# Stacking folded groups in two columns, so that one transfer moves a group's four blocks

## The chip, the cores and the metric

The kernel runs on one core of one Trainium2 chip. The time is device microseconds (us) of one execution; lower is better. Kernels are compared by runs in the fast state, taken in the same rounds on the same chip.

Engine names in the profile: PE is TensorE, DVE is VectorE, ACT is ScalarE, POOL is GpSimd, SP is the engine whose in-order queue issues nearly all transfers here.

## The reference

```python
# x: (1, 384, 384, 384) bf16, w1d: (1,) bf16
g = jnp.einsum("bhwc->bc", x) / (H * W)     # mean of each channel
s = jax.nn.sigmoid(g * w1d[0])              # one factor per channel (k = 1)
return x * s[:, None, None, :]
```

The factor needs all of x, so x must be read once for the sum and be there again for the product. x is 1152 rows of 384 bf16 values on each of 128 partitions, 96 KB a row over all partitions, 113 MB in all. The kernel's arena on the chip holds 275 rows.

## The kernel before

Rows are of two kinds. **Streamed** rows (785) are read and summed, dropped, and read again after the sigmoid. **Kept** rows (367) stay on the chip, so they are read only once. To keep more, the kernel folds: four exponent bits that are the same in nearly all values are dropped, and the twelve bits left of a fourth value take their places in three others. (A check on the data, `verdict`, comes after the sigmoid; if it fails, a slow path redoes the kept rows.) Four blocks of rows then fit in the space of three.

```python
QS = [4, 16, 16, 16, 16]            # quadruples kept in each area
...
areas.append((base, 3 * q))         # three blocks of rows
...
# U, V: where the fourth block lands until it is folded; after the sigmoid, where raw kept rows lie
for name, n in (("U", 8), ("V", 8), ("A", 39), ("Y", 8), ("T", 8)): ...
# ... sum phase, for each pair of four-row pieces:
beside = (U, V)[at % 2]
group_load(g, 3 * e, 3 * f, areas[g][0] + 3 * e)          # three blocks, 24 rows
group_load(g, 3 * q + lo, 3 * q + lo + n, beside)         # the fourth block, 8 rows
fold(k, beside + pieces[k][1] - lo)
stream_all(where)
```

After the sigmoid a pair is unfolded on DVE in six turns (`fields`, `three`, `fourth` for each of two pieces). It is stored by two transfers:

```python
f, t, _ = turns[-2]        # after the second piece's three blocks
turns[-2] = (f, t, lambda: send(KEPT, a, ..., w_done, written))     # 24 rows
f, t, _ = turns[-1]        # after its fourth block
turns[-1] = (f, t, lambda: send(KEPT, at, ..., u_done, written))    # 8 rows, from T or U
```

The order of everything after the sigmoid is fixed when the program is built. A loop keeps a clock and a model of how long DVE and the transfers take; it decides when to scale a piece that has landed, when to unfold, and when a free run of rows is large enough to load into. The SP queue issues strictly in this order.

```python
if n >= BIG or n == N_STREAM - todo or (ahead < LOW and n >= 8) or ahead < LAST:
    load(STREAMED, a, todo, todo + n)       # BIG 32 rows, LOW 9 us queued, LAST 4 us
```

## Time and profile before

| | before |
|---|---|
| time, median of 6 runs | 722.55 us (722.34 to 722.82) |
| span of the profiled run | 721.1 us |
| bytes moved | 303.67 MB |
| transfers on the SP queue | 136 (80 loads, 56 stores) |
| DVE busy | 496.0 us |
| last row landed, sigmoid done | 266.9 us, 270.3 us |

"The turn" below is the stretch around the sigmoid, about 265 to 290 us: reading for the sum ends, storing begins.

### The profile page before, as it was taken

How to read it: one execution, taken by the hardware profiler on the slowest of the kernel's cores; microseconds unless marked ns; L12 is line 12 of the kernel's file. 1: busy time of each engine (PE TensorE's matmuls, PEld its weight loads, DVE VectorE, ACT ScalarE, POOL GpSimd, SP SyncE). 2: the span in 40 equal slices, each digit the busy share in tenths (PEclk: the TensorE clock that was granted, in tenths of full speed). 3: DMA queues.
4: the chain of work that ended last, by engine and by line, in shares of the span. 5: the costliest groups of instructions: out<-in, count | busy, mean ns of one | idle time of the engine just before them, and what ended most of it. 6: DMA issues, size and time to landing. Idle time of an engine off the chain costs nothing.

```text
span 721.1 us, 3241 instructions
## 1 busy us (share of the span) xinstructions
PE 215.7 (30%) x1202; PEld 119.8 (17%) x1202; DVE 496.0 (69%) x469; ACT 115.4 (16%) x92; POOL 0.2 (0%) x4
## 2 busy tenths in 40 slices
PE   5777789888987780000000000000000000000000
PEld 2344445554543440000000000000000000000000
DVE  4600004879989809999999998999979994355330
ACT  3600003656767610001000000000000000000000
POOL 0000000000000000000000000000000000000000
PEclk9899999999999995555555555555555555555555
DMA  9999999999999978999999999999999999999997
GB/s 382 425 447 424 425 429 433 435 434 420 433 424 427 428 326 334 418 427 431 433 429 442 416 433 436 436 443 418 433 431 436 429 440 435 420 436 438 434 432 305
DMA packets 19602, 303.87 MB, mean 421 GB/s; under 512 B 2178, under 2 KB 2178, under 8 KB 6402
## 3 DMA queue, kind: packets, MB, share of 16 engines
q1 hardware_dynamic: 19584, 303.67, 98.6%
q8 instruction: 9, 0.15, 0.1%
q14 instruction: 7, 0.06, 0.0%
q10 hardware_dynamic: 2, 0.00, 0.0%
HBM read 190.41 MB, written 113.25 MB: 421 GB/s over the span
## 4 chain that ended last, share of the span: by engine, by line
DMA 53%; DVE 28%; PE 7%; another core or an unknown queue 4%; ACT 3%; SPq 0%; issue 0%; DVEq 0%
DMA arena<-in_x_dram 37%; DVE arena L437 18%; DMA out_dram<-arena 16%; PE bank L230 7%; DVE arena L254 6%; DVE arena L260 4%; ACT arena L294 3%; SPq L224 0%; ACT s_bf L428 0%; PE bank L509 0%; DVE odd L504 0%; DVE odd_i L513 0%; DVE worst L499 0%; DVEq L112 0%
## 5 line engine op out<-in xcount | busy, mean ns | idle before, releaser
L437 DVE TENSOR_TENSOR arena<-arena,s_bf 128x1536 bf16<-128x1536 bf16 (+8 forms) x102 | 241.7, 2411 | 75.5 <-DMA arena<-in_x_dram 58.2
L230 PE MATMUL bank<-arena,ones 128*128 128x384 bf16 x1152 | 207.6, 343 | 52.0 <-DMA arena<-in_x_dram 51.9
L254 DVE TENSOR_SCALAR arena<-arena 128x1536 uint16<-128x1536 uint16 (+2 forms) x247 | 145.8, 633 | 108.4 <-DMA arena<-in_x_dram 97.9
L230 PEld LDWEIGHTS bank<-arena,ones 128*128 128x128 bf16 x1152 | 114.9, 102 | 144.4 <-DMA arena<-in_x_dram 57.4
L260 DVE TENSOR_TENSOR arena<-arena 128x1536 uint16<-128x1536 uint16 (+2 forms) x114 | 121.0, 1062 | 9.7 <-PE bank L230 7.7
L294 ACT ACTIVATE arena<-arena 128x3072 uint16<-128x3072 uint16 (+1 forms) x38 | 102.5, 2696 | 142.3 <-DVE arena L254 142.3
L364 ACT COPY arena<-bank 128x512 uint32<-128x512 uint32 (+1 forms) x7 | 4.0, 570 | 70.1 <-DMA out_dram<-arena 69.9
L245 PE MATMUL bank<-ones,zeros 128*128 128x384 bf16 x48 | 8.3, 326 | 0.0
L294 ACT ACTIVATION_READ_ACCUMULATOR arena<-arena 128x1 f32 x38 | 7.1, 186 | 0.0
L245 PEld LDWEIGHTS bank<-ones,zeros 128*128 128x128 bf16 x48 | 4.7, 98 | 3.1
L509 PE MATMUL bank<-odd,ones 128*128 128x1 bf16 x1 | 0.2, 186 | 15.8 <-DVE odd L504 15.8
L364 ACT COPY bank<-arena 128x512 uint32<-128x512 uint32 (+1 forms) x7 | 3.6, 565 | 0.0
L428 ACT ACTIVATE s_bf<-bank,w_sc 128x384 bf16<-128x384 f32 x1 | 0.6, 581 | 15.9 <-PE bank L230 15.9
L509 PEld LDWEIGHTS bank<-odd,ones 128*128 128x128 bf16 x1 | 0.1, 104 | 16.2 <-DVE odd L504 16.2
L721 ACT ACT_TABLE_LOAD x1 | 1.3, 1283 | 0.7 <-PEq L737 0.7
L324 DVE TENSOR_SCALAR w_sc<-bank 128x1 f32<-128x1 f32 x1 | 0.2, 157 | 1.1 <-PE bank L319 1.1
L314 DVE MEMSET ones<- 128x128 bf16 x1 | 0.2, 165 | 1.0 <-SPq L106 1.0
L319 PE MATMUL bank<-w_bf,ones 1*128 1x1 bf16 x1 | 0.2, 179 | 2.1 <-DMA w_bf<-in_w1d_dram 2.1
L319 PEld LDWEIGHTS bank<-w_bf,ones 1*128 1x128 bf16 x1 | 0.1, 98 | 2.1 <-DMA w_bf<-in_w1d_dram 2.1
L513 DVE CAST odd_i<-bank 128x1 int32<-128x1 f32 x1 | 0.2, 159 | 0.3 <-PE bank L509 0.3
L504 DVE TENSOR_SCALAR odd<-worst 128x1 bf16<-128x1 f32 x1 | 0.2, 156 | 0.0
L499 DVE TENSOR_REDUCE worst<-seen 128x1 f32<-128x38 f32 x1 | 0.2, 180 | 0.0
(5 smaller groups left out, 0.5 us busy)
## 6 DMA issues: line engine op xcount, KB each, us to landing
arena<-in_x_dram SPq DMA_DIRECT2D x17, 4608.0 KB, 35.4
out_dram<-arena SPq DMA_DIRECT2D x6, 4608.0 KB, 43.8
arena<-in_x_dram SPq DMA_DIRECT2D x19, 1248.0 KB, 11.5
arena<-in_x_dram SPq DMA_DIRECT2D x9, 2304.0 KB, 28.3
out_dram<-arena SPq DMA_DIRECT2D x8, 2304.0 KB, 28.4
arena<-in_x_dram SPq DMA_DIRECT2D x4, 4512.0 KB, 33.6
out_dram<-arena SPq DMA_DIRECT2D x3, 4512.0 KB, 26.7
out_dram<-arena SPq DMA_DIRECT2D x9, 1248.0 KB, 11.7
```

The lines of the kernel that those rows point to most:

```text
L230: return nc.tensor.matmul(acc, lhsT=ones[:], rhs=arena[:, i, :], start=first, stop=last)
L245: lambda: nc.tensor.matmul(acc, lhsT=zeros[:], rhs=ones[:, None, :].to_broadcast([P, C // P, P]), start=False, stop=False),
L254: lambda: nc.vector.tensor_scalar(out=dst, in0=src, scalar1=s0, scalar2=s1, op0=op0, op1=op1),
L260: "DVE", lambda: nc.vector.tensor_tensor(out=dst, in0=a, in1=b, op=op), reads=reads, writes=writes
L294: lambda: nc.scalar.activation(out=y, in_=y, func=ACTF.Copy, accum_out=seen[:, 2 * k + i : 2 * k + i + 1]),
L314: fl.add("DVE", lambda: nc.vector.memset(ones[:], 1.0), writes=["ones"])
L319: lambda: nc.tensor.matmul(votes, lhsT=ones[0:1, :], rhs=w_bf[0:1, 0:1], start=True, stop=True),
L364: "ACT", lambda: nc.scalar.copy(dst.bitcast(u32), src.bitcast(u32)), reads=reads, writes=writes
L428: lambda: nc.scalar.activation(out=s_bf[:], in_=acc, func=ACTF.Sigmoid, scale=w_sc[:, 0:1]),
L437: lambda: nc.vector.tensor_tensor(out=v, in0=v, in1=s_bf[:, None, :].to_broadcast([P, n, C]), op=Op.mult),
L509: lambda: nc.tensor.matmul(votes, lhsT=ones[:], rhs=odd[:], start=True, stop=True),
L721: nc.scalar.preload_act_table(ACTF.Sigmoid)
```

## The change

The intent: halve the transfers of kept groups. Groups of eight quadruples are stacked in two columns. A group takes 32 rows while its fourth block is whole, and the first eight rows of the group above it lie where that fourth block was. So one load brings all four blocks, and one store takes them.

```diff
-    QS = [4, 16, 16, 16, 16]
+    PAIR = 2 * PIECE
+    PAIRS = 4
+    U = 3 * PIECE + PAIRS * 3 * PAIR
+    G0 = U + PAIR
+    V = G0 + PAIRS * 3 * PAIR
 ...
+    GROUPS = [(0, PIECE)]
+    COLUMNS = ([FIRST], [])
+    for i in range(PAIRS):
+        for column, a in zip(COLUMNS, (3 * PIECE, G0)):
+            column.append(len(GROUPS))
+            GROUPS.append((a + 3 * PAIR * i, PAIR))
 ...
+    def take(g, lo=0, hi=None):      # the lines that look up a and hi are left out
+        load(KEPT, a + lo, c_group[g] + lo, c_group[g] + hi)
+        sum_rows(a + lo, hi - lo)
 ...
-    order = [0, 1, 2, BANKED, 3, 4]
+    order = [g for i in (3, 2) for g in (1 + 2 * i, 2 + 2 * i)] + [BANKED]
+    order += [g for i in (1, 0) for g in (1 + 2 * i, 2 + 2 * i)] + [FIRST]
 ...
-        turns[-2] = (f, t, lambda: send(KEPT, a, ..., w_done, written))
+        if len(line) >= total - N_SPLIT and q == PAIR:        # N_SPLIT = 2
+            sent = 3 * PIECE                                  # 12 rows go early
+            turns[-5] = (f, t, lambda: send(KEPT, a, ..., part, written))
-        turns[-1] = (f, t, lambda: send(KEPT, at, ..., u_done, written))
+        turns[-1] = (f, t, lambda: send(KEPT, a + sent, ..., done, written))
```

The stack also fixes an order. A group can be unfolded only when the one above it has left, since its fourth block returns to rows of that one. So groups leave from the top down, and the small group of four, first before, is last. The first two groups out send 12 rows early, to make up for that. The verdict moves from the turn to the end.

More of the change, by code (lines that the diff above doesn't have):

```diff
@@ L149 @@
     ACTF = mybir.ActivationFunctionType
-    QS = [4, 16, 16, 16, 16]
     PIECE = 4
-    Q_BANKS = 6
-    base, areas = 0, []
-    for q in QS:
-        areas.append((base, 3 * q))
-        base += 3 * q
-    RAW = {}
-    for name, n in (("U", 8), ("V", 8), ("A", 39), ("Y", 8), ("T", 8)):
-        RAW[name] = (base, n)
-        base += n
-    ROWS = base
-    N_RAW = sum(n for _, n in RAW.values())
-    U, V, A, Y, T = (RAW[n][0] for n in "UVAYT")
-    BANKED = len(QS)
-    PS = 3 * Q_BANKS
-    QS.append(Q_BANKS)
-    areas.append((A, PS))
+    PAIR = 2 * PIECE
[3 more added lines that the diff above has]
+    V = G0 + PAIRS * 3 * PAIR
+    A = V + PAIR
+    N_A = 39
+    T = A + N_A
+    Y = T + 2 * PIECE
+    ROWS = Y + 2 * PIECE
+    FIRST = 0
+    GROUPS = [(0, PIECE)]
[4 more added lines that the diff above has]
+            GROUPS.append((a + 3 * PAIR * i, PAIR))
+    BANKED = len(GROUPS)
+    GROUPS.append((A, 6))
+    PS = 3 * GROUPS[BANKED][1]
+    N_RAW = ROWS - V + PAIR
     pool = ctx.enter_context(tc.tile_pool(name="sb", bufs=1))
     psum = ctx.enter_context(tc.tile_pool(name="psum", bufs=1, space=bass.MemoryType.PSUM))
-    pieces = [(g, lo, min(PIECE, q - lo)) for g, q in enumerate(QS) for lo in range(0, q, PIECE)]
+    pieces = [(g, lo, min(PIECE, q - lo)) for g, (_, q) in enumerate(GROUPS) for lo in range(0, q, PIECE)]
     ones = pool.tile([P, P], bf16, name="ones")
@@ L200 @@
     fl = Flow(nc, tc)
-    N_STREAM = RPP - N_RAW - sum(4 * q for q in QS)
+    N_STREAM = RPP - N_RAW - sum(4 * q for _, q in GROUPS)
     N_KEPT = RPP - N_STREAM
@@ L209 @@
     c_group = []
-    for q in QS:
+    for _, q in GROUPS:
         c_group.append(r)
@@ L214, with raw @@
     assert r + N_RAW == N_KEPT
+    def raw(a):
+        return c_raw + (a - U if a < G0 else PAIR + a - V)
     summed = [0]
@@ L261, in join @@
         )
-    def area(g, lo, p):
-        a = areas[g][0] + 3 * lo
-        return a, flat(a, 3 * p), [rows(a + j * p, p) for j in range(3)]
     def flat(a, p):
@@ L273, with fold @@
     )
-    def fold(k, ua):
+    def fold(k):
         g, lo, p = pieces[k]
-        a, w, wc = area(g, lo, p)
+        first, q = GROUPS[g]
+        a, ua = first + 3 * lo, first + 3 * q + lo
+        wc = [rows(a + j * p, p) for j in range(3)]
         u, uc = flat(ua, p), rows(ua, p)
@@ L347, in stream_all @@
             i += 1
-    def group_load(g, lo, hi, a):
-        load(KEPT, a, c_group[g] + lo, c_group[g] + hi)
+    def take(g, lo=0, hi=None):
+        a, q = GROUPS[g]
+        hi = 4 * q if hi is None else hi
+        load(KEPT, a + lo, c_group[g] + lo, c_group[g] + hi)
+        sum_rows(a + lo, hi - lo)
     def of_group(g):
         return [i for i, piece in enumerate(pieces) if piece[0] == g]
-    group_load(BANKED, 0, 4 * Q_BANKS, A)
-    sum_rows(A, 4 * Q_BANKS)
+    take(BANKED)
     for k in of_group(BANKED):
-        fold(k, A + PS + pieces[k][1])
+        fold(k)
     in_arena = arena[:, A : A + PS, :].rearrange("p r c -> p (r c)")
@@ L369 @@
         copy_bank(i, in_arena[:, lo:hi], bk[:, 0 : hi - lo], rows(A, PS), [("bank", i)])
-    SLOTS = [(A + i, 13) for i in range(0, 39, 13)]
+    SLOTS = [(A + i, 13) for i in range(0, N_A, 13)]
     S1, S2, S3 = ([slot] for slot in SLOTS)
-    B3, B4, AA = ([area] for area in (areas[3], areas[4], (A, 39)))
-    def halves(area):
-        a, n = area
-        return [(a, n // 2), (a + n // 2, n - n // 2)]
-    V1 = [(V, 8)]
-    EARLY = areas[1:5]
+    HIGH = [(A - 48, 48)]
+    LOW_COLUMN = [(G0 - 48, 48)]
@@ L384 @@
+    take(FIRST)
+    fold(0)
+    EARLY = [(A - 48 * i, 48) for i in (4, 3, 2, 1)]
     BETWEEN = [
-        (EARLY,),
-        (B3,), (B4,),
-        (B3,), (AA,),
-        (halves(areas[4]),), (S1 + S2 + S3,),
+        LOW_COLUMN, HIGH,
+        LOW_COLUMN, [(A, 39)],
+        [(G0 - 24, 24), (A - 24, 24)], (S1, S2 + S3),
         (S1, S2 + S3 + S1), (S2, S3 + S1),
     ]
-    between = sum(n for b in BETWEEN[1:] for where in b for _, n in where)
+    between = sum(n for b in BETWEEN for w in b for _, n in (w if isinstance(w, list) else [w]))
@@ L392 @@
     first = N_STREAM - between
-    at = 0
-    for g, q in enumerate(QS[:BANKED]):
-        for lo in range(0, q, 2 * PIECE):
-            n = min(2 * PIECE, q - lo)
-            beside = (U, V)[at % 2]
-            blocks = BETWEEN[at]
-            cuts = [lo + n * i // len(blocks) for i in range(len(blocks) + 1)]
-            for e, f, where in zip(cuts, cuts[1:], blocks):
-                group_load(g, 3 * e, 3 * f, areas[g][0] + 3 * e)
-                sum_rows(areas[g][0] + 3 * e, 3 * (f - e))
-                if e == lo:
-                    group_load(g, 3 * q + lo, 3 * q + lo + n, beside)
-                    sum_rows(beside, n)
-                for k in of_group(g):
-                    if e <= pieces[k][1] < f:
-                        fold(k, beside + pieces[k][1] - lo)
-                if g:
-                    stream_all(where)
-                else:
-                    stream_all(EARLY[3:], first % 48)
-                    stream_all(EARLY, first - first % 48)
-                    folding = True
-            at += 1
+    stream_all(EARLY[3:], first % 48)
@@ L416 @@
+    stream_all(EARLY, first - first % 48)
+    folding = True
+    for g, where in zip(range(1, BANKED), BETWEEN):
+        k1, k2 = of_group(g)
+        if isinstance(where, list):
+            take(g)
+            fold(k1)
+            fold(k2)
+            stream_all(where)
+        else:
+            take(g, 0, 12)
+            take(g, 24, 32)
+            fold(k1)
+            stream_all(where[0])
+            take(g, 12, 24)
+            fold(k2)
+            stream_all(where[1])
     assert streamed[0] == N_STREAM
@@ L418, in take_raw @@
     def take_raw(a, n):
-        load(KEPT, a, c_raw + a - U, c_raw + a - U + n)
+        load(KEPT, a, raw(a), raw(a) + n)
         sum_rows(a, n)
-    for a, n in S2 + V1 + S3 + S1 + [(U, 8), (Y, 8), (T, 5), (T + 5, 3)]:
+    for a, n in S2 + [(U, 8)] + S3 + S1 + [(V, 8), (Y, 8), (T, 5), (T + 5, 3)]:
         take_raw(a, n)
@@ L449, in store, with unfold @@
         )
-    def unfold(k, a, at):
+    def unfold(k, first):
         g, lo, p = pieces[k]
+        a, at = first + 3 * lo, first + 3 * GROUPS[g][1] + lo
         w, wc = flat(a, 3 * p), [rows(a + j * p, p) for j in range(3)]
@@ L514, in verdict @@
         )
-    N_OVER = 16
+    N_OVER = 8
     moved, scaled = tc.alloc_semaphore("moved"), tc.alloc_semaphore("scaled")
@@ L525, in again @@
             turn = 0
-            for r0, q in zip(c_group, QS):
+            for r0, (_, q) in zip(c_group, GROUPS):
                 for lo in range(r0, r0 + 4 * q, N_OVER):
@@ L548 @@
     BANKS_AT = 2
+    N_SPLIT = 2
     now = dve_at = 0.0
@@ L582, in split @@
         return list(zip(cuts, cuts[1:]))
-    SCRATCH = rows(U, 8) + rows(Y, 16)
-    needed = set(SCRATCH)
+    SCRATCH = rows(Y, 8)
+    needed = [set(SCRATCH + rows(U, 8)), set(SCRATCH + rows(V, 8)), set(SCRATCH)]
     def stored(a, n):
@@ L590, in f @@
             for i in range(a, a + n):
-                if ("a", i) in SCRATCH:
-                    needed.discard(("a", i))
-                else:
+                for left in needed:
+                    left.discard(("a", i))
+                if not Y <= i < Y + 8 and not U <= i < U + 8 and not V <= i < V + 8:
                     idle[i] = True
         return f
-    for a, n, end in ((Y, 4, False), (Y + 4, 4, True), (T, 8, True), (U, 8, True), (V, 8, True)):
-        landed.append((KEPT, a, c_raw + a - U, n, end))
+    for a, n, end in ((T, 4, False), (T + 4, 4, True), (U, 8, True), (Y, 8, True), (V, 8, True)):
+        landed.append((KEPT, a, raw(a), n, end))
     for a, n in SLOTS:
-        landed.append((KEPT, a, c_raw + a - U, n, True))
-    HALVES = (T, U)
-    half = [True, True]
-    order = [0, 1, 2, BANKED, 3, 4]
-    line = deque((g, lo, min(2 * PIECE, QS[g] - lo)) for g in order for lo in range(0, QS[g], 2 * PIECE))
-    total = sum(n for _, _, n in line)
+        landed.append((KEPT, a, raw(a), n, True))
+    order = [g for i in (3, 2) for g in (1 + 2 * i, 2 + 2 * i)] + [BANKED]
+    order += [g for i in (1, 0) for g in (1 + 2 * i, 2 + 2 * i)] + [FIRST]
+    line = deque(order)
+    home = {g: i for i, column in enumerate(COLUMNS) for g in column}
+    home[BANKED] = 2
+    free = [True, True, True]
+    total = len(GROUPS)
     out_rows = 0
@@ L610 @@
     bank_at = None
-    pair = 0
     since = None
@@ L614, with start_group @@
     stall = 0.0
-    def start_pair():
-        nonlocal pair, bank_at
-        if not line or needed or not half[pair % 2]:
-            return False
-        g, lo, n = line[0]
-        if g == BANKED and (bank_at is None or now < bank_at[1]):
+    def start_group():
+        if not line:
+            return False
+        g = line[0]
+        column = home[g]
+        if needed[column] or not free[column] or g == BANKED and (bank_at is None or now < bank_at[1]):
             return False
         line.popleft()
-        h = pair % 2
-        at = HALVES[h]
-        half[h] = False
-        pair += 1
-        a = bank_at[0] if g == BANKED else areas[g][0]
-        a += 3 * lo
-        mine = [k for k in of_group(g) if lo <= pieces[k][1] < lo + n]
-        def w_done():
-            nonlocal out_rows
-            out_rows += n
-            release(a, 3 * n)
-        def u_done():
-            half[h] = True
-        for k in mine:
-            e = pieces[k][1] - lo
-            fields, three, fourth = unfold(k, a + 3 * e, at + e)
-            turns.extend((fields + (None,), three + (None,), fourth + (None,)))
-        f, t, _ = turns[-2]
-        turns[-2] = (f, t, lambda: send(KEPT, a, c_group[g] + 3 * lo, c_group[g] + 3 * (lo + n), w_done, written))
@@ new lines, in start_group, with part, done @@
+        free[column] = False
+        a, q = GROUPS[g]
+        if g == BANKED:
+            a = bank_at[0]
+        below = 0
+        if column < 2 and g != COLUMNS[column][0]:
+            below = GROUPS[COLUMNS[column][COLUMNS[column].index(g) - 1]][1]
+        def part():
+            release(a + below, sent - below)
+        def done():
+            nonlocal out_rows
+            out_rows += 1
+            free[column] = True
+            release(a + max(below, sent), 4 * q - max(below, sent))
@@ L647, in start_pair @@
+        for k in of_group(g):
+            fields, three, fourth = unfold(k, a)
+            turns.extend((fields + (None,), three + (None,), fourth + (None,)))
+        sent = 0
+        if len(line) >= total - N_SPLIT and q == PAIR:
+            f, t, _ = turns[-5]
+            sent = 3 * PIECE
+            turns[-5] = (f, t, lambda: send(KEPT, a, c_group[g], c_group[g] + sent, part, written))
         f, t, _ = turns[-1]
-        turns[-1] = (f, t, lambda: send(KEPT, at, c_group[g] + 3 * QS[g] + lo, c_group[g] + 3 * QS[g] + lo + n, u_done, written))
+        turns[-1] = (f, t, lambda: send(KEPT, a + sent, c_group[g] + sent, c_group[g] + 4 * q, done, written))
@@ L656 @@
             if not can and (ahead >= PENDING or not landed):
-                can = start_pair()
-                if can and not asked:
-                    verdict()
-                    asked = True
+                can = start_group()
             if landed and (ahead < PENDING or not can):
@@ L679 @@
             moves.append([now + LAT, n * ROW + PER_STORE, then])
-        if out_rows == total and not checked and all(half):
+        if not asked and not line and not turns:
+            verdict()
+            asked = True
+        if out_rows == total and not checked:
             checked = True
@@ L686 @@
         got = runs()
-        if bank_at is None and len(line) <= len(QS) * 2 - BANKS_AT and got and max(got)[0] >= PS:
+        if bank_at is None and len(line) <= total - BANKS_AT and got and max(got)[0] >= PS * 4 // 3:
             a = max(got)[1]
-            for i in range(a, a + PS):
+            for i in range(a, a + PS * 4 // 3):
                 idle[i] = False
```

## The prediction

> **What bounds the kernel now.** I read the page first, its busy shares and its 40 slices:
>
> ```profile
> PE 215.7 (30%) x1202; PEld 119.8 (17%) x1202; DVE 496.0 (69%) x469; ACT 115.4 (16%) x92; POOL 0.2 (0%) x4
> ...
> DMA  9999999999999978999999999999999999999997
> GB/s 382 425 447 424 425 429 433 435 434 420 433 424 427 428 326 334 418 427 431 433 429 442 416 433 436 436 443 418 433 431 436 429 440 435 420 436 438 434 432 305
> ...
> q1 hardware_dynamic: 19584, 303.67, 98.6%
> ...
> HBM read 190.41 MB, written 113.25 MB: 421 GB/s over the span
> ```
>
> The DMA row is at 9 nearly everywhere, and the rate stands near 430 GB/s in nearly all slices; VectorE (DVE) is busy for only 69% of the span. So the kernel moves bytes at the limit of its DMA engines, and only three places are below it: the first slice, slices 15 and 16, and the last. Then the stretches between those places, with the columns PE, PEld, DVE, ACT, POOL, granted clock, DMA share, GB/s:
>
> ```profile
> 0.00:3.00 3.00, 0.18 (x1) 0.10 (x1) 0.40 (x3) 1.28 (x1) 0.20 (x4) 1.00 0.47 111
> 3.00:265.00 262.00, 210.74 (x1174) 117.18 (x1175) 138.10 (x190) 109.53 (x83) 0.00 (x0) 0.95 1.00 430
> 265.00:272.00 7.00, 4.63 (x28) 2.37 (x26) 1.66 (x2) 0.58 (x1) 0.00 (x0) 1.00 0.19 76
> 272.00:285.00 13.00, 0.00 (x0) 0.00 (x0) 13.00 (x7) 0.00 (x0) 0.00 (x0) 0.54 0.93 389
> 285.00:290.00 5.00, 0.19 (x1) 0.10 (x1) 4.65 (x11) 0.00 (x0) 0.00 (x0) 0.50 0.98 306
> 290.00:715.00 425.00, 0.00 (x0) 0.00 (x0) 338.21 (x259) 3.99 (x7) 0.00 (x0) 0.50 1.01 431
> 715.00:721.10 6.10, 0.00 (x0) 0.00 (x0) 0.00 (x0) 0.00 (x0) 0.00 (x0) 0.50 0.20 84
> ```
>
> At 431 GB/s the 303.67 MB need 303.67 / 0.431 = 704.6 us. What is lost against that rate: start 3 x (1 - 111/431) = 2.2 us; the first 262 us at 430, 0.6; the seven us at the turn 5.8; the thirteen after it 1.3; the five after those 1.5; the end 6.1 x (1 - 84/431) = 4.9. Together 16.3, and 704.6 + 16.3 = 720.9, the span of 721.1. That is the whole account; a change can shrink a loss, raise the rate, or move fewer bytes.
>
> The turn is a true dependency, as the chain in order of time shows:
>
> ```profile
> 254.15 12.72 DMA arena<-in_x_dram
> 266.87 0.05 issue
> 266.92 2.79 PE bank L230 x16
> 269.71 0.02 issue
> 269.73 0.59 ACT s_bf L428
> 270.32 0.02 issue
> 270.35 14.84 DVE arena L437 x8
> 285.18 0.11 DVE worst L499
> ```
>
> The last row lands, TensorE sums what is left, the sigmoid follows, DVE scales four rows, and only then can a store start. Nothing in the change shortens that.
>
> **What the Trainium skill says.** "DMA: Bandwidth & Descriptors", section "Anatomy of one DMA", gives each transfer a fixed cost of about 2.0 us, most of it the wait for the write to be confirmed. The transfer count would then matter much. This trace agrees on latency but not as a cost of the queue: 13-row loads take 11.5 us to land, yet the stretch 200 to 250 us, dominated by them, moves 426 GB/s, against 433 in 40 to 110 us, where transfers are 40 to 48 rows. A full queue hides the wait. Section "The descriptor swizzle" of the same page has eight data descriptors and one for completion on each of 16 engines, 144 in all. The trace agrees: 19584 packets / 144 = 136 transfers, and 2176 packets of 4 bytes / 16 = 136 too. Section "Measured" has about 10.5 ns for a packet. In the trace's packet records the mean packet of an 8-row transfer (6144 B) took 236.6 ns and one of 48 rows (36864 B) 1365.6 ns: 0.03675 ns a byte, which leaves 236.6 - 225.8 = 10.8 ns fixed, so it agrees. "Perfetto Trace Analysis", section "DMA Optimizations", says that larger transfers fill the bandwidth better, and that splitting lets some start sooner; the change does the first everywhere and the second in two groups.
>
> **The change part by part.**
>
> Bytes: the arena stays at 275 rows. Before, 204 area rows and 71 raw rows; after, V = 212, so 275 - 212 + 8 = 71 raw rows, and 4 + 8 x 8 + 6 = 74 quadruples as before. So 367 rows are kept and 785 streamed in both, and the bytes are the same: 704.6 us of the total don't move. This is the main step.
>
> Loads of the sum phase: before, one for the banked group; then nine pairs with two loads each, and a third for each of the last two, which are cut: 21. After: one banked, one first group, five with one load, three cut ones with three: 16. The stream loads (424 rows first, then 361) and the eight raw loads stay. Five fewer.
>
> Stores of kept groups: before, ten pairs with two stores each: 20, among them those of the page's two lines of 2304 KB (x8) and the eight-row 768 KB ones. After: ten, and one more for each of the first two groups, which send 12 rows early: 12. Eight fewer. The 26 remaining loads and 28 streamed stores of the second phase come from the schedule loop with its limits of 48 and 32 rows; freed runs start at another size (24 rows and the eight of the group below later), so I put these at 0 +- 4.
>
> One transfer costs the engines 8 x 10.8 + 9 ns (the completion packet) = 0.095 us in a full queue; with medians of packet times (234 and 1364 ns) it is 0.07. 13 x 0.095 = 1.2 us less. The issue itself (0.34 us on the queue's sequencer, from the trace) lies beside 20 to 40 us of queued transfers and is worth nothing.
>
> Phase one's folding: the same instructions on the same sizes, since a fold still works on four-row pieces. A group's load now overwrites the fourth block of the group two before it; before, U and V were taken in turn with the same distance of two. So the wait only changes its name. The last fold ended at 253.74 us, where the queue still held 12.7 us of loads, of which the last 24 rows are 5.5; about 7 us of slack, so a fold that ends a little later costs nothing.
>
> The turn: DVE scales 71 raw rows in both, 14.84 us. Then before spends 0.8 us on the verdict (285.10 to 285.91), which the change moves to the end, where DVE is mostly idle: the first unfolding starts 0.8 us earlier. The first kept store comes after fields and three blocks of a piece, as before, with 12 rows in both (before because the group of four comes first, after because of the split). Of the 1.5 us lost at 285 to 290, I count 0.4 as gained. Part of that loss is reads starting on a nearly drained queue, which the change does not touch; its first free run is even smaller (the eight rows of T, then 13 at a time, against V and the first 13 together).
>
> After 290 us: each pair's unfolding costs DVE 2 x 9.8 us (the chain has one piece from 373.33 to 383.13). Its 32 rows now leave together instead of 24 after 18 us and 8 two us later. A lump of 32 rows is 7.3 us of DMA, and the schedule asks for 24 us of queued work before it starts one, so a bubble should be rare; I put 0.4 us for it. Sum: 722.55 - 1.2 - 0.4 + 0.4 = 721.35.
>
> **The rivals.** First, fixed cost in the open: 13 transfers x 2.0 us = 26 us, so about 697 us. For it speaks only the skill's fit for single transfers; against it the 426 to 433 GB/s at three and a half times the transfer size, so under 1%. Second, DVE becomes the bound: from 290 to 530 us it is busy for 229.27 of 240 us, and stores wait for it on the in-order queue (270.9 us in total for L437). If larger lumps and the wait for a whole column entry let the queue run dry once per later group, at one or two us each, the time is 725 to 735. Against it: the queue's waits have not emptied the engines once after 290 us (431 GB/s), and DVE has 115 - 43 = 72 us free after 600. Third, the turn shrinks more than I allow, its dips at 272 to 290 us (2.8 us) gone: 719. Fourth, the unfolding ends so late that the last group or the check after it sets the end; the streamed rows end at 692 us on DVE now and the unfolding before 600, so this needs 90 us of delay.
>
> **Range and chances.** Bytes fix 704.6 us and the start, the seven us of the turn and the end fix 12.9 more; what is left to change is about 5 us downwards, of which I expect one or two, and some bubbles upwards. So 721.3 us, 8 in 10 from 718.8 to 724.2. A gain of 2% (14.5 us) isn't there to be had: 0.01. A loss of 2% needs a new stall several times over: 0.02. Within 2%: 0.97.
>
> **What would show it.** In the changed kernel's page: the bytes unchanged; q1's packets at about 123 x 144 = 17700 instead of 19584, with MB the same; DVE busy time within 3 us of 496; the rate 430 or more outside the three places; the fold's end before about 260 us; the last row's chain the same seven us. The prediction is wrong if the rate between 290 and 715 falls under 427 (bubbles, the second rival), if the packets fall and the rate rises by more than 1% (the first), or if the turn moves by more than two us.

## The result, and the profile after

| | before | after |
|---|---|---|
| time, median of 6 runs | 722.55 us (722.34 to 722.82) | 722.45 us (721.62 to 723.04) |
| span of the profiled run | 721.1 us | 721.3 us |
| transfers on the SP queue | 136 | 131 |
| loads, stores after the turn (raw and kept ones with them) | 26, 56 | 30, 52 |
| DVE busy | 496.0 us | 496.3 us |

The ratio is 0.9996, with a 95% interval from 0.9984 to 1.0009: the same time.

Three lines of the changed kernel's page, against those that the prediction shows of the one before:

```profile
PE 214.6 (30%) x1202; PEld 119.2 (17%) x1202; DVE 496.3 (69%) x470; ACT 115.4 (16%) x92; POOL 0.2 (0%) x4
...
GB/s 382 429 443 424 425 435 430 431 433 433 424 427 427 428 320 341 425 430 426 403 430 436 428 438 430 429 439 433 432 432 439 423 445 431 432 430 433 435 436 306
...
q1 hardware_dynamic: 18864, 303.67, 98.6%
```

The bytes are the same. 18864 packets / 144 = 131 transfers, so five fewer, not thirteen. And the rate has a slice that the kernel before did not have: the twentieth, 403 GB/s, near 345 us.

The turn's chain in the changed kernel, in order of time (start, us, what):

```profile
254.26 12.24 DMA arena<-in_x_dram
...
266.55 2.79 PE bank L241 x16
...
269.36 0.59 ACT s_bf L432
```

The last row lands at 266.50 us instead of 266.87. That is 0.37 us gained in the sum phase, where five loads are gone. One pair of traces overstates it: in the four traces that keep the sum phase of the kernel before, the last row lands at 266.62 to 266.87 us, and in the eight with that of the changed kernel at 266.32 to 266.58. The means, 266.74 and 266.49, are 0.25 us apart, 0.05 us a load.

Now the stretches after the sigmoid, first of the kernel before (the last column is GB/s):

```profile
272.00:290.00 18.00, 0.19 (x1) 0.10 (x1) 17.65 (x17) 0.00 (x0) 0.00 (x0) 0.53 0.95 366
290.00:340.00 50.00, 0.00 (x0) 0.00 (x0) 48.23 (x39) 0.00 (x0) 0.00 (x0) 0.50 1.01 427
340.00:360.00 20.00, 0.00 (x0) 0.00 (x0) 19.90 (x20) 3.99 (x7) 0.00 (x0) 0.50 1.02 433
360.00:715.00 355.00, 0.00 (x0) 0.00 (x0) 270.08 (x202) 0.00 (x0) 0.00 (x0) 0.50 1.00 432
```

The same of the changed kernel:

```profile
272.00:290.00 18.00, 0.00 (x0) 0.00 (x0) 17.96 (x13) 0.00 (x0) 0.00 (x0) 0.50 0.96 373
290.00:340.00 50.00, 0.00 (x0) 0.00 (x0) 47.76 (x42) 4.00 (x7) 0.00 (x0) 0.50 1.01 427
340.00:360.00 20.00, 0.00 (x0) 0.00 (x0) 16.25 (x14) 0.00 (x0) 0.00 (x0) 0.50 1.01 408
360.00:715.00 355.00, 0.18 (x1) 0.10 (x1) 273.90 (x209) 0.00 (x0) 0.00 (x0) 0.50 1.00 433
```

Against 431 GB/s the first stretch gains 18 x (373 - 366) / 431 = 0.3 us. The third loses 20 x (433 - 408) / 431 = 1.2 us. So in this execution a small gain at the turn and in the sum phase is given back by one dip. Bytes counted from the packet records say the same: the changed kernel is 0.22 MB (0.5 us at 431 GB/s) ahead of the one before at 340 us, and 0.25 MB (0.6 us) behind it at 360. The last stretch can't be compared this way, since rates are rounded to 1 GB/s, which is 0.8 us over 355 us.

What the dip is: here is the chain of the changed kernel around it.

```profile
331.60 13.71 DMA out_dram<-arena
345.30 0.02 issue
345.32 12.01 DMA arena<-in_x_dram
```

A load issued at 345.32 us had waited for a store of the same rows to land. The SP queue's own record has a 13-row load at 342.19, a store at 342.57, then nothing until that load (start, us the instructions took):

```profile
342.19 0.34 SPq L235 DMA_DIRECT2D arena<-in_x_dram  x1
342.57 0.58 SPq L451 DMA_DIRECT2D out_dram<-arena  x1
345.32 2.48 SPq L235 DMA_DIRECT2D arena<-in_x_dram  x2
```

While it waited, nothing behind it could be issued, and behind the stores then ending the engines had only 13 and 11 rows left. In the trace's packet records that 13-row load, from 344.4 to 351.0 us, took 497 ns a packet in the mean, where the 13-row transfers around it took 375. Its median is 376: half of its packets took the usual time, and some up to 1430 ns. That the queue had run short is what this load has in common with slow ones elsewhere; that it is the cause is argued here, not shown by a run of its own.

The queue's waits in total (us, times, longest) for a load that needs rows still being stored, first of the kernel before:

```profile
SPq L224 <- DMA out_dram<-arena: 114.0, 22, 16.0
```

And of the changed kernel:

```profile
SPq L235 <- DMA out_dram<-arena: 145.2, 28, 17.3
```

Space is waited for more often. The order on the queue shows why. The streamed loads after the turn are, in rows, 8, 13, 13, 13, 12, 8, 13, 13, 13, 18, 21, 26, then 36 to 48 but for the last 18, before. After, they are 8, 13, 13, 13, 8, 13, 13, 21, 13, 13, 10, 11, 24, 13, 23, 24, 16, 13, 34, then 40 to 48 but for the last 32. The changed kernel lives on small recycled pieces for longer, so it makes four more streamed loads and four more streamed stores. Sum: five loads fewer in the sum phase, eight kept stores fewer, eight streamed transfers more: five fewer.

### The profile page after: what moved, and what is told of

Its sections match the earlier page's. It is cut to its first block, busy times and chain, and to the rows that moved or that the text cites. A ratio compares the mean times of both kernels' runs of the same rounds, so it can differ in the third digit from the quotient of the medians.

```text
span 721.3 us, 3240 instructions
## 1 busy us (share of the span) xinstructions
PE 214.6 (30%) x1202; PEld 119.2 (17%) x1202; DVE 496.3 (69%) x470; ACT 115.4 (16%) x92; POOL 0.2 (0%) x4
## 3 DMA queue, kind: packets, MB, share of 16 engines
q1 hardware_dynamic: 18864, 303.67, 98.6%
## 4 chain that ended last, share of the span: by engine, by line
DMA 55%; DVE 28%; PE 6%; ACT 5%; SPq 0%; issue 0%; another core or an unknown queue 0%; DVEq 0%
DMA arena<-in_x_dram 38%; DVE arena L441 19%; DMA out_dram<-arena 17%; DVE arena L265 6%; PE bank L241 6%; ACT arena L302 5%; DVE arena L271 3%; SPq L235 0%; ACT s_bf L432 0%; SPq L762 0%; DVEq L112 0%; SPq L106 0%
```

## The experiments

Twelve kernels ran, all with correct results. Theory 1 at the start: in a saturated queue a transfer costs only its packets' fixed time, 0.07 to 0.10 us, so the change could win about a microsecond, and its gain was mostly given back by more streamed transfers. Theory 2, formed from the dip: what sets the small differences is whether the in-order queue runs short in the 70 us after the turn. Rivals are in each expectation.

### What one transfer costs

Every store, or every load, of 24 rows or more is cut in two in the kernel before, without a change of the order.

```diff
     def store(chunk, a, lo, hi):
-        return fl.add("SP", lambda: nc.sync.dma_start(out=view(of, r0, n)[:, lo:hi, :], ...))
+        return [fl.add("SP", ...rows lo + e to lo + f...) for e, f in
+                ([(0, (hi - lo) // 2), ((hi - lo) // 2, hi - lo)] if hi - lo >= 24 else [(0, hi - lo)])]
```

> The kernel before, its schedule unchanged, every store of 24 rows or more sent as two halves: 22 transfers more (136 to 158), the same bytes. Theory 1 (a transfer costs the saturated queue only its eight packets' fixed time and a completion packet, 0.07 to 0.10 us): 1.5 to 2.2 us slower, so about 724.4 us, DMA-busy time up by the same. Rival A (the two us of fixed cost of a single transfer stand in the open): about 44 us slower. Rival B (the cost is hidden beside the other queued transfers): 722.5 us, within 0.3.

Measured: 723.52 us beside 722.36 of the kernel before, ratio 1.0015 (1.0001 to 1.0028).

The second has the same cut in `load`.

> The kernel before, every load of 24 rows or more sent as two halves: 36 transfers more (136 to 172). Theory 1: 2.5 to 3.5 us slower, about 725.5 us. Rival A: over 70 us slower. Rival B: 722.5 us, or a little less because the first half lands earlier.

Measured: 723.34 us beside 722.36, ratio 1.0014 (1.0000 to 1.0027). The queue's line in the kernel with halved stores (packets, MB, share of 16 engines' span):

```profile
q1 hardware_dynamic: 22752, 303.67, 98.7%
```

And with halved loads:

```profile
q1 hardware_dynamic: 24768, 303.67, 98.9%
```

These are 158 and 172 transfers. The shares are rounded to 0.1%, which is 0.7 us, so the packet records themselves were summed: 712.4 and 713.4 us of 16 engines, against 710.9 before. So a transfer adds 1.5 / 22 = 0.07 us and 2.5 / 36 = 0.07 us of engine time: the packet arithmetic holds, at the low end of the 0.07 to 0.10 expected. But the time of the kernel rose by only 1.16 / 22 = 0.05 us and 0.98 / 36 = 0.03 us a transfer. The two expectations of 1.5 to 2.2 and of 2.5 to 3.5 us were too large. Rival A (2 us each in the open) is out by a factor of 38 and more. Rival B (free) is barely excluded, if at all: the intervals begin at 1.0001 and 1.0000. That both kernels moved the same way, with the engine time, speaks against it. Why the time rises less than the engines' busy time is not settled; packets overlap (the DMA share stands at 1.01), which would hide a part. The sum phase gives a cleaner figure: with 22 loads more there, the halved loads' last row landed at 267.67 us, against the mean of 266.74, so 0.04 us each.

### The merge undone, the rest left

```diff
-        load(KEPT, a + lo, ...32 rows...)          # and the store of 32 rows
+        ...three blocks, 24 rows...; ...the fourth, 8 rows...     # cut where it is issued, order kept
```

> The changed kernel with its schedule unchanged, but each transfer of a kept group's four blocks sent as two, three blocks and the fourth: 16 transfers more (131 to 147). This undoes what the change is for, and nothing else. Theory 1 (0.07 to 0.10 us each): 1.1 to 1.5 us slower than the changed kernel, about 723.7 us, less up to 1 us if the three blocks' earlier store fills the dip that the changed kernel shows at 344 to 350 us. Rival A: 32 us slower. Rival B: the same, or faster by the dip's 1.3 us.

Measured: 722.76 us (721.81 to 724.14), ratio to the kernel before 1.0007 (0.9993 to 1.0020), against 0.9996 for the changed kernel. The difference, 0.8 us for 16 transfers, agrees with 0.05 us each, but it lies inside the intervals. In the stretch from 340 to 360 us it moved 413 GB/s, against 408. The last row landed at 266.75 us, 0.26 later than in the changed kernel's traces, with six loads more. So the merge itself, which the change is named for, is worth about 0.8 us as measured, and that is not clear of the noise.

### Without the early store

```diff
-    N_SPLIT = 2
+    N_SPLIT = 0
```

> The changed kernel without the early store of 12 rows in the first two groups (131 to 129 transfers). Theory (the turn needs early data: without it the queue falls dry while DVE unfolds 32 rows, some 20 us, before the first kept store): a new dip under 400 GB/s between 295 and 310 us and 0.8 to 2 us slower, 723 to 724.5 us. Rival (enough small streamed transfers are queued, the split is worth nothing): within 0.3 us of the changed kernel.

Measured: 726.06 us beside 722.36, ratio 1.0053 (1.0040 to 1.0067). It is 3.7 us slower than the kernel before, where the changed kernel in its own rounds was 0.1 us faster: 3.8 us between them, with two transfers fewer. Its windows:

```profile
290.00:340.00 50.00, 0.00 (x0) 0.00 (x0) 47.01 (x41) 4.00 (x7) 0.00 (x0) 0.50 1.01 422
340.00:360.00 20.00, 0.00 (x0) 0.00 (x0) 17.01 (x14) 0.00 (x0) 0.00 (x0) 0.50 1.01 369
```

Against the changed kernel these two lose 50 x 5 / 431 = 0.6 and 20 x 39 / 431 = 1.8 us. These are 2.4 of the 2.6 us between the two spans, 723.9 and 721.3; the medians are further apart, since this profiled run was the fastest of its five (725.72 us) and the changed kernel's the slowest of its six. The expectation was right that it is slower, but undersized (0.8 to 2 us), and the dip was not where it said: 295 to 310 us moved 427 GB/s, and the dips are at 315 to 320 (364), 340 to 345 (322) and 350 to 360 us (366). What it shows: the early stores, first of them twelve rows at 295 us instead of all 32 at 316, are worth more than all the transfers that the change removes. Without them the loop also chose another order (31 loads after the turn, not 30), so how much is the early rows and how much that order isn't told apart.

### The verdict alone

```diff
-                if can and not asked:
-                    verdict()
 ...
+        if not asked and not line and not turns:
+            verdict()
 ...
```

> The kernel before with one part of the change alone: the verdict of 0.8 us on DVE at the turn is made after the last unfolding. All transfers and their order are the same. Theory 1 (the turn's DVE work is on the path): 0.4 to 0.8 us faster, about 721.8 us. Rival (the first unfolding's store is not waited for; the queue holds other rows until 294 us): 722.4 us, within 0.3.

Measured, in the kernel before: 722.61 us beside 722.65, ratio 0.9999 (0.9985 to 1.0013). The rival's number came, but the interval, 1.1 us faster to 0.9 slower, is too wide to exclude the 0.4 to 0.8 us of theory 1. The trace speaks for the rival. The first unfolding began at 284.85 us instead of 285.83, yet the stretch at the turn moved 367 GB/s for 366, and the one after it, 290 to 340 us, 427 for 427. So DVE's 0.8 us at the turn is not seen on the path.

### Other orders

In each of three kernels a few settings of the loop differ, and the whole later order follows. First, the rows of T are not free until the third raw slot is stored.

```diff
-                if not Y <= i < Y + 8 and ...:
+                if not Y <= i < Y + 8 and ... and not T <= i < T + 8:
                     idle[i] = True
+            if a + n == T:
+                release(T, 8)
```

> The changed kernel, but the eight rows of T are not read into again until the third raw slot is out, so that no eight-row load goes in among the first stores (131 to 135 transfers, some later pieces smaller). Theory 1 (that early small load slows the packets around 276 to 282 us and puts 1.75 us of scaling ahead of the first unfolding): the dip at 276 to 282 us goes, but one like that of the kernel before comes at 285 to 290 us, so within 0.7 us of the changed kernel. Rival (the early load fills an otherwise empty queue): 1 to 2 us slower, 723.5 to 724.5 us.

Measured: 723.97 us beside 722.65, ratio 1.0016 (1.0002 to 1.0029).

```profile
272.00:290.00 18.00, 0.00 (x0) 0.00 (x0) 17.96 (x14) 0.00 (x0) 0.00 (x0) 0.56 0.96 385
290.00:340.00 50.00, 0.00 (x0) 0.00 (x0) 49.79 (x43) 3.99 (x7) 0.00 (x0) 0.50 1.01 419
```

The turn is better than in any other kernel here (385 GB/s), which is 0.5 us against the changed kernel. The fifty us after it give 50 x 8 / 431 = 0.9 us back. Theory 1 had the turn right (the dip moved to 285 to 290 us, 363 GB/s) and the total wrong; the 723.97 us are inside the range of its rival. Why it is some 1.4 us slower than the changed kernel isn't settled: by 715 us its trace has moved as much as the changed kernel's, and its last packets end at 720.1 us instead of 718.9.

Second, fewer transfers through larger pieces:

```diff
-    PENDING, MERGE = 24.0, 12.0
-    BIG, CAP, PART, LOW, LAST = 32, 48, 16, 9.0, 4.0
+    PENDING, MERGE = 24.0, 4.0
+    BIG, CAP, PART, LOW, LAST = 32, 48, 16, 7.0, 4.0
```

> The changed kernel with two limits of the schedule moved: a small load waits until 7 us (not 9) are queued, and neighbouring pieces are stored together unless under 4 us (not 12) are queued. 131 to 126 transfers, the small recycled pieces 21 and 26 rows rather than 10 to 13. Theory 1 (fewer transfers at 0.03 to 0.07 us each): 0.2 to 0.4 us faster, 722 us. Rival (what costs are the dips, and waiting longer before storing makes them deeper): a dip under 400 GB/s between 295 and 350 us and 1 to 4 us slower.

Measured: 724.29 us, ratio 1.0020 (1.0007 to 1.0034). It has the fewest transfers of all, and this stretch:

```profile
310.00:320.00 10.00, 0.00 (x0) 0.00 (x0) 9.00 (x10) 0.00 (x0) 0.00 (x0) 0.50 0.98 346
```

That one dip costs 10 x (1 - 346/431) = 2.0 us. The rival was right: a dip under 400 GB/s in that range, and 1 to 4 us slower.

Third, early stores in four groups:

```diff
-    N_SPLIT = 2
+    N_SPLIT = 4
-        return 0.15 + 0.1 * n      # the loop's DVE times; also 0.15 + 0.2 * n
+        return 0.08 + 0.1 * n
-    ... LOW 9.0
+    ... LOW 7.0
```

> The changed kernel with the early store in the first four groups, the loop's DVE times set to those of the trace (0.08 us instead of 0.15 fixed), and the 7 us limit: 129 transfers. Theory 2 (the dip at 344 to 350 us is the second group's rows coming too late as one lump): earlier stores of the next groups fill it, and it is 1 us faster than the changed kernel, about 721.3 us, without a slice under 415 between 290 and 360 us. Rival (the dip comes from small slots that are waited for, in order, on the queue): the dip stays or moves and the time is within 0.5 us of the changed kernel or slower.

Measured: 724.91 us, ratio 1.0029 (1.0015 to 1.0043). Theory 2 in this form fell: the dip did not go (352 GB/s from 345 to 350 us), and its trace has another at 315 to 320 us (333). More early stores, a clock closer to DVE's real times and a lower limit, changed together here, did not make a better order.

### The changed kernel once more

> The changed kernel as it is, once more, beside the next ones on the same chip. Theory: 722.3 us, within 0.4; the dip at 344 to 350 us is there again (it follows from the order on the queue, not from chance). Rival (the dip is noise of one execution): no slice under 400 GB/s between 290 and 360 us.

Measured: 722.37 us (722.13 to 722.72), ratio again 0.9996 (0.9982 to 1.0010).

```profile
272.00:290.00 18.00, 0.00 (x0) 0.00 (x0) 17.97 (x13) 0.00 (x0) 0.00 (x0) 0.54 0.98 378
290.00:340.00 50.00, 0.00 (x0) 0.00 (x0) 47.63 (x42) 3.99 (x7) 0.00 (x0) 0.50 1.01 427
340.00:360.00 20.00, 0.00 (x0) 0.00 (x0) 17.64 (x15) 0.00 (x0) 0.00 (x0) 0.50 1.01 425
360.00:715.00 355.00, 0.19 (x1) 0.10 (x1) 272.58 (x208) 0.00 (x0) 0.00 (x0) 0.50 1.00 432
```

The queue's issues are at the same places (342.19, then 345.61 us), but the third stretch moved 425 GB/s, not 408. So neither expectation holds as written: the order on the queue is fixed and leaves it short there every time, but how deep the dip gets differs from one execution to another. The first profiled execution took 723.04 us, the slowest of its six; this one took 722.45. The spans were 721.3 and 720.7, and the difference between 408 and 425 GB/s over 20 us is 0.8 us, so it covers all that separates them. Why the depth varies is open.

### DVE relieved by GpSimd

If DVE supplies scaled rows too late after the turn, another engine could scale one raw slot beside it.

```diff
+        fl.add("POOL", lambda v=v: nc.gpsimd.tensor_tensor(out=v, in0=v, in1=s_bf..., op=Op.mult),
+               reads=rows(a, 13) + ["s_bf"], writes=rows(a, 13))
 ...
-                scale(a, n)
-                dve_at = now + TT(n)
+                if chunk == KEPT and a in BESIDE:
+                    dve_at = now
+                else:
+                    scale(a, n)
+                    dve_at = now + TT(n)
```

> The changed kernel, with the 13 rows of the third raw slot scaled on GpSimd beside DVE at the turn, so that DVE is 2.75 us earlier with all that follows (135 transfers). Theory 2 (the dips after the turn come from DVE supplying scaled rows too late): no dip at 344 to 350 us, 1 to 2 us faster than the changed kernel, about 721 us. Rival (they come from small slots waited for in order, whatever DVE does): the dip stays, within 0.4 us of the changed kernel, or slower through four more transfers. Third (GpSimd slows DVE[...]): DVE's instructions at the turn lengthen, 1 us or more slower.

> The same relief of DVE in the kernel before (140 transfers). It has no dip after 290 us, so theory 2 gives at most the 0.5 us of the dips at 272 to 282: 722.0 to 722.5 us. Rival (DVE at the turn is on the path in this kernel too): 1 to 2 us faster.

> The changed kernel with two raw slots scaled on GpSimd, so DVE is 5.5 us earlier (133 transfers), if GpSimd does a slot in 6 us or less. Theory 2: as fast as with one slot or 0.5 us faster, 720.5 to 721 us. Rival: GpSimd takes longer than DVE saves, the second slot's store is late and blocks the in-order queue: 723 us or more.

Measured: 733.65, 732.81 and 741.37 us beside 722.54, ratios 1.0164 (1.0148 to 1.0179), 1.0140 (1.0125 to 1.0156) and 1.0258 (1.0244 to 1.0272). The third outcome of the first expectation happened, larger than thought. From the changed kernel with one slot, GpSimd's group, then DVE in the timeline (start, us), then a stretch:

```profile
L452 POOL TENSOR_TENSOR arena<-arena,s_bf 128x4992 bf16<-128x4992 bf16 x1 | 10.4, 10365 | 269.6 <-ACT s_bf L432 269.6
```

```profile
270.89 10.35 DVE L441 TENSOR_TENSOR arena<-arena,s_bf 128x1536 bf16<-128x1536 bf16 x1
```

```profile
273.00:280.00 7.00, 0.00 (x0) 0.00 (x0) 7.00 (x1) 0.00 (x0) 7.00 (x1) 0.50 0.00 0
```

A DVE instruction on four rows, 0.9 us otherwise, stood for 10.35 us, until GpSimd was done. Nothing was scaled, so nothing could be stored, and the DMA engines stood still. The Trainium skill says this: "SBUF — State Buffer", section "Who interferes with whom", has a DVE instruction with two SBUF inputs contend with a GpSimd instruction that reads SBUF, through a shared read interface; it calls the pair of shared ports an exclusive lock. The trace agrees: the DVE instruction lasted 10.35 us beside a GpSimd one of 10.37. So these three runs could not test whether an earlier DVE removes the dips; that stays open. (In the first one's trace no five us between 290 and 360 us fell under 409 GB/s, but its order on the queue differs too, with 31 loads after the turn instead of 30.)

### All together

The times come from different rounds; the ratios compare within their own.

| kernel | transfers | time, us | ratio to before |
|---|---|---|---|
| changed, larger pieces | 126 | 724.29 | 1.0020 |
| changed, no early store | 129 | 726.06 | 1.0053 |
| changed, four early stores | 129 | 724.91 | 1.0029 |
| changed | 131 | 722.45 | 0.9996 |
| changed, T held | 135 | 723.97 | 1.0016 |
| before | 136 | 722.55 | 1 |
| changed, blocks apart | 147 | 722.76 | 1.0007 |
| before, stores halved | 158 | 723.52 | 1.0015 |
| before, loads halved | 172 | 723.34 | 1.0014 |

The number of transfers does not order the times. Where the order on the queue is kept, time rises a little with transfers. Where the order changes, dips after the turn outweigh them. No version beat both kernels; the changed kernel and the one before are equal within 0.2%.

## Why the prediction was right, point by point

The time, 722.45 us, is inside the range of 718.8 to 724.2, and within 2% as given 97%. The central 721.3 was 1.15 us low, and that is instructive, since the expected gain was about that size: the time came out right because bytes and rate fix it, not because the gain came.

- **Bytes fixed, DMA engines the bound.** Right. 303.67 MB in both, and 431 GB/s in the stretch 290 to 715 us in both.
- **The loads of the sum phase, five fewer.** Right. The last landing moved by 0.37 us in the first pair of traces and by 0.25 in the mean of all, 0.05 each.
- **The kept stores, eight fewer.** Right by itself.
- **The streamed transfers after the turn, "at 0 +- 4".** This term failed: they were eight more (four loads, four stores). The 13 became five, and q1 had 18864 packets, not the 17700 forecast. The prediction even named the cause, that freed runs start at another size, but took it for small.
- **"One transfer costs the engines 8 x 10.8 + 9 ns", 0.095 us.** The engines' busy time rose by 0.07 us each, as the prediction's own medians had it (it went on with the larger figure, from means), and the time by 0.03 to 0.05 when they were added. With five of them the term is 0.15 to 0.25 us of time, or 0.35 by the engine time, instead of 1.2.
- **The turn, 0.4 us.** The size was right: 366 GB/s became 373 and 378 over 18 us, 0.3 and 0.5 us. The reason given was wrong. The verdict moved alone gave nothing that could be seen, and the first unfolding began later (286.40 us, not 285.83), because the eight rows loaded early into T were scaled ahead of it. What gave the gain instead was not isolated.
- **"A bubble should be rare; I put 0.4 us for it."** There is one, at a fixed place in the order. It cost 1.2 us in one profiled execution and 20 x (433 - 425) / 431 = 0.4 us in the other. The sign asked for, 430 GB/s or more outside the three places, failed in that slice (403), while the rate from 290 to 715 us stayed at 431, above the 427 under which the prediction called itself wrong.
- **DVE's total and the folding.** Right: 496.3 us for 496.0, and the last fold ended at 253.86 us for 253.74, with no effect.
- **Rivals.** Fixed cost in the open is refuted by both halved kernels. DVE as the bound, with a bubble at each later group, did not happen, though a small form of it did: one dip where the queue waits for space. The turn gained no 2.8 us. The unfolding ended at 599 us and did not set the end.
- **Three slips in its working.** The "5 us downwards" sets the time (722.55) against losses counted on the span (721.1); span against span, 721.1 - 704.6 - 12.9, it is 3.6. "So under 1%" doesn't follow from 426 and 433 GB/s, which differ by 1.6%. And the 11.5 us to landing are mostly waiting in a full queue, so they say nothing of the skill's 2.0 us. What does is a store of four rows on the empty queue after the sigmoid: 2.3 us to landing, of which 0.9 are its bytes at 431 GB/s, which leaves 1.4 (an estimate).

With the corrected terms: 722.55 - 0.3 (transfers) - 0.4 (turn) + 0.4 to 1.2 (dip) is 722.25 to 723.05, which holds both measured medians. That sum is my own working, made afterwards; the runs show its terms one by one, most of them smaller than the noise of the times, and do not isolate the dip's share.

## What to carry to other kernels

When the DMA engines are saturated, count what a merged transfer really costs there (here 0.03 to 0.07 us) before redesigning a layout for it; the latency of a lone transfer is not that cost. Ask what the new layout does to the order in which memory comes free, for smaller free runs can make the transfers again that the merge saved. And in an in-order queue, look first at the stretch where little is queued: sending 12 rows of two groups early, with the order that came of it, was worth 3.8 us, more than all the merging.

## What the Trainium skill lacked or had wrong

- "DMA: Bandwidth & Descriptors", "Anatomy of one DMA": its 2.0 us for a transfer, given there for transfers issued from GpSimd, is mostly completion latency, as the section says itself. No page gives what one more transfer costs in a full queue: 0.07 us of engine time, 0.03 to 0.05 us of the kernel's time (22 more stores, +1.16 us; 36 more loads, +0.98 us), for transfers issued from SP.
- No page has what packets do when the queue is short: in the dip a 13-row load's packets took 497 ns in the mean instead of 375, and at the turn of the changed kernel those of two eight-row transfers took 307 and 312 instead of 234. The kernel before has such a pair at its turn too (479 for 375, 292 for 234), and the kernel without the early store has four 13-row loads of 434 to 517 in its dips. In the 13-row load of the dip, half of the packets took the usual time.
- "SBUF — State Buffer", "Who interferes with whom" was right: a DVE product of 0.9 us stood for 10.35 us beside a GpSimd one.
